# Turned pairs' first parts issued one tile later and behind the split, one block per turned copy, and the turned copy read ahead of the MLP's weights

## The chip, the cores and the metric

One NeuronCore of one Trainium2 chip runs the whole program. The metric is the device time of one execution in microseconds (us). Engines as the profile names them: PE is TensorE (matmuls and transposes by matmul), PEld its weight loads, DVE is VectorE, ACT is ScalarE, POOL is GpSimd, SP is SyncE, whose queue starts nearly all of this kernel's DMAs.

## The reference, cut to what matters

Two layers; in each, an FNet Fourier sublayer and an MLP, both with a LayerNorm ahead of them (the MLP with two, one inside the other).

```python
S, D, F = 2048, 576, 4608
def _A_ref(x, dft_seq_re, dft_seq_im, dft_hid_re, dft_hid_im):
    a = jnp.einsum("bsd,ed->bse", x, dft_hid_re)
    b = jnp.einsum("bsd,ed->bse", x, dft_hid_im)
    return jnp.einsum("ts,bse->bte", dft_seq_re, a) - jnp.einsum("ts,bse->bte", dft_seq_im, b)
def _B_ref(x, w1, b1, w2, b2):
    y = _layernorm(x)
    h = _gelu(jnp.einsum("bsd,df->bsf", y, w1) + b1)
    return jnp.einsum("bsf,fd->bsd", h, w2) + b2
x = A_x
for layer in range(2):
    x = x + _A_ref(_layernorm(x), ...)
    x = x + _B_ref(_layernorm(x), ...)
```

## The kernel before, in words

Every float32 product is made of three passes over a high and a low part of each operand (`PASSES`); "splitting" a tile is a copy to the high part on ACT and a subtraction for the low part on DVE (`split`). The large products use a seven-product block scheme (Strassen and Winograd's), so that sums of blocks are made ahead of the multiplication.

The order of all work is the order in which the program's lines run: there is no scheduler. Each engine has one queue and takes its instructions in that order; an instruction whose operand is not ready holds up all that stands behind it on its engine. SP's queue holds the DMA starts in the same way.

A layer has four parts one after the other: the sequence DFT, then for each half of the 2048 rows a **hidden stage** (function `hidden`: the hidden DFT, the residual sum, the norms and the turning of the result) and the MLP of that half (`mlp`). The hidden stage so occurs four times in the program. All that is changed is in it.

A hidden stage has eight tiles n = 0 to 7 of 128 rows. For a tile it

- loads the sequence DFT's result of tile n+2 (`h.load`, DMA `uv_mid`) and x;
- splits tile n+1 (`turn`, line 202 on ACT, 1152 columns, and line 199 on DVE): PE needs the high part for a tile's first four matmuls and the low part from the fifth on;
- lets PE run 54 matmuls (9 blocks k, 3 passes, 2 halves; line 209);
- adds the sum to x (line 196 on DVE), and makes the norm: `norms(n)` is a generator of three steps, the statistics (DVE, then POOL's lines 230 to 234), the normalising (line 253 on ACT), and adding b2 to x (line 196 on POOL). The caller places its steps with `next(ln)`: the second and the third stand in the next tile's iteration.

The MLP needs the normalised tiles turned (columns in partitions) and in seven block combinations, split again, in the array `y`. Tiles go in pairs j: tiles 0 and 1 (j = 0), 2 and 3 (j = 1), 4 and 5 (j = 2), and 6 and 7 by themselves. The ways of turning differ:

- Pairs 0 and 1 go **through DRAM**. `write_turned(j)` at the start of tile 2 or 4 transposes 32 by 32 blocks on DVE (line 206) and writes the block `raw` to DRAM (`y_mid`, two DMAs); `read_turned(j)` in tile 3 or 5 at k = 1 reads it back with four DMAs in another order. Then `first_parts(j)` makes the three combinations that are plain blocks (line 985: three copies on ACT, and five subtractions of line 199 on DVE), `turn_sums(j)` makes the block sums (four subtractions on POOL, in place), and `turn_parts(j)` the four combinations that are sums (three copies on ACT, three subtractions on DVE).
- Pair 2 is turned **by PE**: `turn_blocks`, called after tile 6, makes 8 transposes (line 959) and 4 more (line 962); then `first_parts(2)` and `turn_sums(2)`, the latter on DVE. PE's transposes of tile 5's blocks need tile 5's normalising.
- Tiles 6 and 7 are turned by PE in `turn_y` (line 1020) after tile 7, with the first part of the MLP's product (35 matmuls of 128x256) ahead of them on PE.

Where things stand in the iterations of the hidden stage before:

```python
                if n in (3, 5):
                    if k == 1:
                        read_turned(n // 2 - 1)
                    if k == 8:
                        first_parts(n // 2 - 1)
                if n in (4, 6):
                    if k == 1:
                        turn_sums(n // 2 - 2)
                    if k == 8:
                        turn_parts(n // 2 - 2)
```

So `first_parts(0)` is issued at the end of tile 3, ahead of tile 3's sum and of the split of tile 5 (start of tile 4), and `first_parts(1)` at the end of tile 5, ahead of the split of tile 7. The MLP's generator is started at the start of tile 5 (`next(mlp)` at n == NP - 3), which starts the reads of its first weights (`w_parts`): two in the first half of a layer, seven in the second.

The blocks: `t8` and `t9` of 8 x 288 columns each. `raw` is the front of `t8`. Both turned copies are read into `turned_x`, the front of `t9`; pair 2's turned copy lies in `t8` behind column 768. Tiles 4 and 5 are normalised into `t8`, tiles 6 and 7 into `t9`.

Of the kernel before, what the change touches and what calls it, by code (L numbers as in the profile page):

```python
# [15 lines left out]
P = 128  # L16
NT = S // P
DH = D // 2
NP = NT // 2
# [138 lines left out]
def spectral_mixer(ctx: ExitStack, tc: tile.TileContext, x, dh, c0, cs, w1, b1, w2, b2, out):  # L158
# [33 lines left out]
    def dma(dst, src):  # L192
        nc.sync.dma_start(dst, src)  # L193
# [682 lines left out]
    def hidden(h, mlp):  # L876
# [12 lines left out]
        y = Y(7, 5, TC)  # L889
        t8 = A.alloc(8 * DH, low=True)  # L890
        t9 = A.alloc(8 * DH, low=True)
        es, b2t = A.alloc(7 * 3 * 32, low=True), A.alloc(D, low=True)
        raw, turned_x = Block(A, t8.at, 4 * DH), Block(A, t9.at, 12 * P)
        dma(b2t(D), b2.to_broadcast([P, D]))

        def norms(n):

            tile_x = xv[:, :, order[n]]
            if n < 4:
                g = raw(9, 4, 32).rearrange("p g e i -> p e g i")  # L900
# [24 lines left out]
            if n < NP - 1:  # L925
                add(nc.gpsimd, tile_x, tile_x, b2t(2, DH))
            yield
# [8 lines left out]
        def read_turned(j):  # L936
            src = yd[j].rearrange("(q d) c f -> c d q f", q=4)
            for c in range(4):
                dma(turned_x(4, 3 * P)[32 * c:32 * c + 32], src[c])

        def rests(j):
            e = es(7, 3, 32)
            if j == 2:
                v = t8(8, DH)
                nc.scalar.activation(e[:, :4], v[:, 0:4, None, 2 * P:].to_broadcast([P, 4, 3, 32]), AF.Copy)
                return
            v = t9(8, DH)
            nc.scalar.activation(e[:, :, 1].bitcast(F32R), v[:, 1:8, 2 * P:], AF.Copy)
# [3 lines left out]
        def turn_blocks():  # L952


            v, x = t8(8, DH), t8(8 * DH)[:, 6 * P:].rearrange("p (b k t) -> p b k t", b=4, k=3)
            a, b = space(), space()
# [9 lines left out]
        def parts(j, e, i, high=True, low=True, engine=nc.vector):  # L966


            if j < 2:
                x = turned_x(4, 3, 4, 32).rearrange("p q f e t -> p f e q t")[:, :, e]  # L970
                yv = y[:, :, :, j * P:(j + 1) * P].rearrange("p i f (q t) -> p f i q t", q=4)[:, :, i]
# [6 lines left out]
            else:  # L978
                x = t8(8 * DH)[:, 6 * P:].rearrange("p (b k t) -> p b k t", b=4, k=3)[:, e]
                yv = y[:, i, :, j * P:(j + 1) * P]  # L980
# [13 lines left out]
        def turn_sums(j):  # L994
            if j < 2:
                x = turned_x(12, 4, 32).rearrange("p g e t -> p e g t")
            else:
                x = t8(8 * DH)[:, 6 * P:].rearrange("p (b k) -> p b k", b=4)
            b11, b12, b22, b21 = (x[:, k] for k in range(4))
# [9 lines left out]
        def turn_y():  # L1009
            v = t9(8, DH)  # L1010
            at = slice(3 * P, 4 * P)
            blocks = (1, 7, 6, 2, 3, 4, 5)
            for m, i0 in enumerate((2, 4, 0, 6)):
# [21 lines left out]
        for n in range(NP):  # L1035
# [19 lines left out]
            for k in range(KH):  # L1055
                if n == 0 and k == KH // 2:
                    drain(turn(1))
                if n in (3, 5):
                    if k == 1:
                        read_turned(n // 2 - 1)  # L1060
                    if k == 8:
                        first_parts(n // 2 - 1)
                if n in (4, 6):
                    if k == 1:
                        turn_sums(n // 2 - 2)
                    if k == 8:
                        turn_parts(n // 2 - 2)
                if k == 4:
# [33 lines left out]
        add(nc.gpsimd, tile_x, tile_x, b2t(2, DH))  # L1102
        for b in (*h.places, t8, t9, es, b2t):
            b.free()
# [369 lines left out]
```

## Time and profile before

| | |
|---|---|
| median of 3 runs | 2758.68 us (2756.53 to 2760.1) |
| profiled execution | 2756.53 us, the fastest of the three |
| its span, first to last instruction | 2754.7 us (1.8 us lie outside) |
| granted TensorE clock, mean | 0.983 |
| PE busy / DVE / ACT / POOL | 96% / 66% / 40% / 31% |
| idle time of PE ahead of line 959 / line 1020, four stages | 37.2 us / 12.9 us |
| idle time of PE for a low part (DVE line 199), whole program | 27.8 us |

How to read it: a PE at 96% leaves about 4% of gaps, and the program can gain no more from filling them than the gaps and what the lower clock costs behind them. The rows of a timeline are merged runs of equal instructions of one engine: start, duration of the run, engine and line, what is written from what, count, and in brackets the idle time of the engine just before and what ended it. Rows of SPq are DMA starts.

### The profile page before, as it was taken

What the parts mean: (1) busy time and instruction counts of PE and PEld (TensorE: products, weight loads), DVE (VectorE), ACT (ScalarE), POOL (GpSimd) and SP (SyncE); (2) the same over time, 40 slices, a digit from 0 to 9 for tenths busy, and PEclk for the clock granted to TensorE, in tenths of its full rate; (3) what the DMA queues carried; (4) which work ended last, traced back from release to release, by engine and by line L of the source; (5) the groups of instructions that cost most, each with busy time, mean ns of one, the idle gap of its engine ahead of it and who ended that gap; (6) DMA issues with size and microseconds to landing.
All of it is one profiled execution on the core that took longest, in us unless ns stands there. A gap on an engine that the chain in (4) does not pass through costs nothing.

```text
span 2754.7 us, 44664 instructions
## 1 busy us (share of the span) xinstructions
PE 2656.1 (96%) x17156; PEld 2486.7 (90%) x17156; DVE 1820.7 (66%) x2539; ACT 1103.8 (40%) x1817; POOL 845.1 (31%) x730
## 2 busy tenths in 40 slices
PE   9999997999999799999999999979999996999999
PEld 9999997888888788988899999978999996998988
DVE  8999975877776465556677777456555554655555
ACT  6555553544443243333354333334333322433331
POOL 6334334434442332222250000232222233321222
PEclk9999998999999899999999999989999998999999
DMA  5777785777778656666553333746666685666664
GB/s 176 250 251 247 244 269 178 257 269 275 264 270 304 166 157 195 193 202 218 160 207 131 123 125 122 211 140 196 193 192 193 194 260 143 189 193 197 190 197 154
DMA packets 236164, 557.47 MB, mean 202 GB/s; under 512 B 24352, under 2 KB 87840, under 8 KB 235808
## 3 DMA queue, kind: packets, MB, share of 16 engines
q1 hardware_dynamic: 222624, 524.53, 60.9%
q10 hardware_dynamic: 13328, 30.09, 2.9%
q8 instruction: 136, 2.23, 0.3%
q14 instruction: 76, 0.62, 0.1%
HBM read 436.16 MB, written 121.01 MB: 202 GB/s over the span
## 4 chain that ended last, share of the span: by engine, by line
PE 59%; DVE 2%; DMA 1%; SPq 1%; issue 1%; ACT 0%; POOL 0%; DVEq 0%; POOLq 0%; ACTq 0%
PE bank L209 59%; DVE R L199 1%; SPq L193 1%; DMA R<-w_parts 0%; DVE A L196 0%; DMA R<-uv_mid 0%; DMA A<-y_mid 0%; PE bank L1020 0%; DVE A L199 0%; POOL moments L230 0%; DVE moments L224 0%; DMA A<-uv_mid 0%; ACT A L253 0%; ACT R L985 0%; PE bank L1030 0%
## 5 line engine op out<-in xcount | busy, mean ns | idle before, releaser
L209 PE MATMUL bank<-R 128*128 128x288 f32 (+2 forms) x16972 | 2625.7, 316 | 40.5 <-DVE R L199 27.8
L209 PEld LDWEIGHTS bank<-R 128*128 128x128 f32 x16972 | 2456.9, 190 | 206.9 <-DVE R L199 33.2
L196 DVE TENSOR_TENSOR A<-bank,A 128x576 f32<-128x576 f32 (+3 forms) x808 | 567.9, 709 | 532.9 <-PE bank L209 439.3
L199 POOL TENSOR_TENSOR R<-A,R 128x512 fp32r<-128x512 f32 (+1 forms) x286 | 373.6, 1317 | 905.1 <-ACT R L1283 866.0
L199 DVE TENSOR_TENSOR R<-A,R 128x1024 fp32r<-128x1024 f32 (+7 forms) x555 | 524.7, 971 | 168.5 <-ACT R L985 123.4
L196 POOL TENSOR_TENSOR A<-A 128x576 f32<-128x576 f32 (+2 forms) x102 | 144.0, 1416 | 526.5 <-ACT A L693 340.5
L199 POOL TENSOR_TENSOR A<-A 128x384 f32<-128x384 f32 (+3 forms) x184 | 226.4, 1234 | 223.1 <-DVE R L199 95.4
L1222 ACT ACTIVATE bank<-bank,b1t 128x512 f32<-128x512 f32 (+1 forms) x224 | 144.9, 647 | 369.4 <-DVE bank L196 242.5
L1283 ACT ACTIVATE R<-A 128x512 fp32r<-128x512 f32 x288 | 177.0, 629 | 271.8 <-DVE A L199 123.6
L652 ACT ACTIVATE R<-A 128x1024 fp32r<-128x1024 f32 x196 | 206.3, 1054 | 106.6 <-PE bank L209 63.7
L196 DVE TENSOR_TENSOR bank<-bank,A 128x512 f32<-128x512 f32 (+1 forms) x228 | 152.3, 669 | 144.2 <-PE bank L209 143.2
L199 DVE TENSOR_TENSOR R<-bank,R 128x512 fp32r<-128x512 f32 x232 | 156.0, 675 | 4.8 <-ACT R L1283 4.2
L199 DVE TENSOR_TENSOR A<-A 128x1024 f32<-128x1024 f32 (+3 forms) x134 | 147.1, 1104 | 4.4
L1283 ACT ACTIVATE R<-bank 128x512 fp32r<-128x512 f32 x216 | 121.3, 595 | 29.9 <-PE bank L209 29.8
L1249 ACT ACTIVATE A<-bank 128x512 f32<-128x512 f32 (+1 forms) x76 | 43.7, 575 | 208.8 <-PE bank L209 208.6
L253 ACT ACTIVATE A<-A,moments 128x576 f32<-128x576 f32 (+2 forms) x90 | 57.6, 689 | 131.0 <-POOL moments L234 93.5
L230 POOL TENSOR_TENSOR moments<-moments,power 128x1 f32<-128x1 f32 x32 | 43.1, 1346 | 191.1 <-DVE moments L227 191.1
L199 DVE TENSOR_TENSOR A<-bank,A 128x512 f32<-128x512 f32 x144 | 97.9, 680 | 0.0
L279 ACT ACTIVATE R<-A 128x256 fp32r<-128x256 f32 x126 | 51.9, 412 | 64.6 <-DMA A<-in_w 19.7
L1222 ACT ACTIVATE A<-bank,b1t 128x512 f32<-128x512 f32 (+1 forms) x76 | 50.6, 666 | 62.6 <-DVE bank L196 62.6
L985 ACT ACTIVATE R<-A 128x384 fp32r<-128x384 f32 (+3 forms) x60 | 35.2, 643 | 90.8 <-DMA A<-y_mid 57.8
L206 DVE STREAM_TRANSPOSE A<-A 128x1152 f32<-128x1152 f32 x40 | 55.1, 1378 | 15.4 <-ACT A L253 12.4
(64 smaller groups left out, 610.4 us busy)
## 6 DMA issues: line engine op xcount, KB each, us to landing
R<-w_parts SPq DMA_DIRECT2D x504, 320.0 KB, 3.4
R<-w_parts SPq DMA_DIRECT2D x189, 576.0 KB, 3.8
A<-in_cs SPq DMA_DIRECT2D x112, 512.0 KB, 4.0
w_parts<-R SPq DMA_DIRECT2D x63, 576.0 KB, 5.0
w_parts<-R ACTq DMA_DIRECT2D x81, 320.0 KB, 3.6
uv_mid<-A SPq DMA_DIRECT2D x28, 576.0 KB, 3.1
w_parts<-R SPq DMA_DIRECT2D x45, 320.0 KB, 4.3
A<-in_w SPq DMA_DIRECT2D x72, 192.0 KB, 4.7
```

The costliest lines, as they stand in the source:

```text
L196: engine.tensor_tensor(dst, a, b, op=op)
L199: engine.tensor_tensor(dst, a, b, op=OP.subtract)
L206: nc.vector.transpose(block(2 * D), block(2 * D))
L209: nc.tensor.matmul(o, a, b, start=start, stop=stop, skip_group_check=True)
L230: nc.gpsimd.tensor_tensor(mv[:, 3:4], mv[:, 2:3], power[:, 0:1], op=OP.pow)
L253: nc.scalar.activation(dst, src, AF.Identity, bias=mv[:, 4:5], scale=mv[:, 3:4])
L279: nc.scalar.activation(t[:, 1:4:2], src[:, 0:3:2], AF.Copy)
L652: nc.scalar.activation(self.cells[t, i](2, NP, P)[:, 0], self.source(t, i), AF.Copy)
L985: nc.scalar.activation(dst, src, AF.Copy)
L1222: nc.scalar.activation(dst, src, AF.Gelu_apprx_tanh, bias=bias(f))
L1249: nc.scalar.activation(up, o, AF.Copy)
L1283: nc.scalar.activation(H[q, k](2, TC)[:, 0], src, AF.Copy)
```

## The change

What it does, in four edits:

1. `first_parts(j)` moves from the end of tile 3 (5) to the start of tile 4 (6), behind the split of tile 5 (7) and ahead of the normalising of tile 3 (5). `turn_sums(j)` moves from k = 1 of tile 4 (6) to just ahead of k = 0, which is the same place on POOL. `turn_parts(j)` moves from the end of tile 4 (6) to the start of tile 5 (7), behind the split of tile 6; for pair 1 there is no split there.
2. The two turned copies that come from DRAM get a block each (`xs[0]`, `xs[1]`); pair 2's copy has the block of pair 0's.
3. Tiles 6 and 7 are normalised into the block in which tiles 4 and 5 lay (`v8`, the front of which is `raw`); the back half of `v8`, for tile 7's sums, lies over pair 1's copy. The room is 4224 columns in place of 4608, so `es` and `b2t`, which are taken next, lie lower.
4. `next(mlp)` moves from the start of tile 5 to its k = 3, behind the DMAs of `read_turned(1)`.

```diff
-        t8 = A.alloc(8 * DH, low=True)
-        t9 = A.alloc(8 * DH, low=True)
+        t8 = A.alloc(4 * DH + 24 * P, low=True)
...
-        raw, turned_x = Block(A, t8.at, 4 * DH), Block(A, t9.at, 12 * P)
+        raw, v8 = Block(A, t8.at, 4 * DH), Block(A, t8.at, 8 * DH)
+        xs = [Block(A, t8.at + 4 * DH + k * 12 * P, 12 * P) for k in (1, 0, 1)]
...
-            elif n < 6:
-                v = t8(8, DH)
+            else:
+                v = v8(8, DH)
                 z = v[:, 0:2] if n % 2 else v[:, 2:4]
-            else:
-                v = t9(8, DH)
-                z = v[:, 0:2] if n % 2 else v[:, 6:8]
...
-                b12, b22, t1, t3, t2, t4, b11, b21 = (v[:, k] for k in range(8))
+                b12, b22, b11, b21, t1, t3, t2, t4 = (v[:, k] for k in range(8))
...
             if n:
                 drain(turn(n + 1))
+                if n in (4, 6):
+                    first_parts(n // 2 - 2)
+                if n in (5, 7):
+                    turn_parts(n // 2 - 2)
                 next(ln)
+                if n in (4, 6):
+                    turn_sums(n // 2 - 2)
             if n in (2, 4):
                 write_turned(n // 2 - 1)
             if n == 6:
                 rests(2)
-            if n == NP - 3:
-                next(mlp)
             o = space()
...
-                if n in (3, 5):
-                    if k == 1:
-                        read_turned(n // 2 - 1)
-                    if k == 8:
-                        first_parts(n // 2 - 1)
-                if n in (4, 6):
-                    if k == 1:
-                        turn_sums(n // 2 - 2)
-                    if k == 8:
-                        turn_parts(n // 2 - 2)
+                if n in (3, 5) and k == 1:
+                    read_turned(n // 2 - 1)
+                if n == NP - 3 and k == 3:
+                    next(mlp)
```

No instruction is added or taken away. What moves in the queues, in the first of the four hidden stages (the others have the same order but for the loads). First ACT, from the normalising of tile 2 to that of tile 5; L253 is normalising, L202 the split's copy (1152 columns), L985 the copies of first parts (3x128) and of turned sums (4x128). Before:

```order
L253 ACTIVATE A<-A,moments 128x2x4x32 x2
L253 ACTIVATE A<-A,moments 128x2x32
L985 ACTIVATE R<-A 128x3x128 x3
L202 ACTIVATE R<-A 128x1152
L253 ACTIVATE A<-A,moments 128x2x4x32 x2
L253 ACTIVATE A<-A,moments 128x64
L985 ACTIVATE R<-A 128x4x128 x3
L202 ACTIVATE R<-A 128x1152
L253 ACTIVATE A<-A,moments 128x576
L985 ACTIVATE R<-A 128x3x128 x3
L202 ACTIVATE R<-A 128x1152
L253 ACTIVATE A<-A,moments 128x576
```

With the change, at the same place on ACT (its line 980 is line 985 of before):

```order
L253 ACTIVATE A<-A,moments 128x2x4x32 x2
L253 ACTIVATE A<-A,moments 128x2x32
L202 ACTIVATE R<-A 128x1152
L980 ACTIVATE R<-A 128x3x128 x3
L253 ACTIVATE A<-A,moments 128x2x4x32 x2
L253 ACTIVATE A<-A,moments 128x64
L202 ACTIVATE R<-A 128x1152
L980 ACTIVATE R<-A 128x4x128 x3
L253 ACTIVATE A<-A,moments 128x576
L202 ACTIVATE R<-A 128x1152
L980 ACTIVATE R<-A 128x3x128 x3
L253 ACTIVATE A<-A,moments 128x576
```

Each group of part copies has changed places with the split that stood behind it. On DVE the subtractions move further, past the residual sum and the statistics too. At DVE's end of the stage, up to tile 7's sum (the last row); L224 to L227 are tile 6's statistics, `A<-A 128x384 x4` is `turn_sums(2)`. Before:

```order
L199 TENSOR_TENSOR R<-A,R 32x4x128
L199 TENSOR_TENSOR R<-A,R 128x4x128 x2
L196 TENSOR_TENSOR A<-bank,A 128x2x288
L224 BN_STATS moments<-A 128x6 x2
L225 BN_AGGR moments<-moments 128x2
L227 TENSOR_SCALAR moments<-moments 128x1
L199 TENSOR_TENSOR R<-A,R 32x2x128
L199 TENSOR_TENSOR R<-A,R 128x2x2x128
L199 TENSOR_TENSOR R<-A,R 32x128
L199 TENSOR_TENSOR R<-A,R 128x2x128
L199 TENSOR_TENSOR A<-A 128x384 x4
L196 TENSOR_TENSOR A<-bank,A 128x2x288
```

With the change, from tile 6's sum to tile 7's:

```order
L196 TENSOR_TENSOR A<-bank,A 128x2x288
L224 BN_STATS moments<-A 128x6 x2
L225 BN_AGGR moments<-moments 128x2
L227 TENSOR_SCALAR moments<-moments 128x1
L199 TENSOR_TENSOR R<-A,R 32x2x128
L199 TENSOR_TENSOR R<-A,R 128x2x2x128
L199 TENSOR_TENSOR R<-A,R 32x128
L199 TENSOR_TENSOR R<-A,R 128x2x128
L199 TENSOR_TENSOR A<-A 128x384 x4
L199 TENSOR_TENSOR R<-A,R 32x4x128
L199 TENSOR_TENSOR R<-A,R 128x4x128 x2
L196 TENSOR_TENSOR A<-bank,A 128x2x288
```

The subtractions of pair 1's turned sums (`32x4x128` and `128x4x128 x2`) have moved from ahead of tile 6's sum to between `turn_sums(2)` and tile 7's sum. Last SP, in tile 5's iteration, behind the write of pair 1's copy and tile 7's loads (`A<-y_mid` is the read of pair 1's copy, `R<-w_parts` the MLP's weights, `dh_parts` the hidden DFT's parts that are kept in DRAM, in the first stage alone):

```order
 L193 DMA A<-in_x 128x2x288
 L193 DMA dh_parts<-R 128x576 x2
-L193 DMA R<-w_parts 128x640 x2
-L193 DMA A<-y_mid 32x4x384 x4
+L193 DMA A<-y_mid 32x4x384 x4
+L193 DMA R<-w_parts 128x640 x2
 L193 DMA dh_parts<-R 128x576 x6
```

The read of the copy and the weights have changed places; in the second half of a layer seven weight reads stand there in place of two.

More of the change, by code (lines that the diff above doesn't have):

```diff
@@ L938, in read_turned @@
             for c in range(4):
-                dma(turned_x(4, 3 * P)[32 * c:32 * c + 32], src[c])
+                dma(xs[j](4, 3 * P)[32 * c:32 * c + 32], src[c])
         def rests(j):
-            e = es(7, 3, 32)
+            e, v = es(7, 3, 32), v8(8, DH)
             if j == 2:
-                v = t8(8, DH)
                 nc.scalar.activation(e[:, :4], v[:, 0:4, None, 2 * P:].to_broadcast([P, 4, 3, 32]), AF.Copy)
                 return
-            v = t9(8, DH)
             nc.scalar.activation(e[:, :, 1].bitcast(F32R), v[:, 1:8, 2 * P:], AF.Copy)
@@ L952, in turn_blocks @@
         def turn_blocks():
-            v, x = t8(8, DH), t8(8 * DH)[:, 6 * P:].rearrange("p (b k t) -> p b k t", b=4, k=3)
+            v, x = raw(4, DH), xs[2](4, 3, P)
             a, b = space(), space()
@@ L978, in parts @@
             else:
-                x = t8(8 * DH)[:, 6 * P:].rearrange("p (b k t) -> p b k t", b=4, k=3)[:, e]
+                x = xs[j](4, 3, P)[:, e]
                 yv = y[:, i, :, j * P:(j + 1) * P]
@@ L995, in turn_sums @@
             if j < 2:
-                x = turned_x(12, 4, 32).rearrange("p g e t -> p e g t")
+                x = xs[j](12, 4, 32).rearrange("p g e t -> p e g t")
             else:
-                x = t8(8 * DH)[:, 6 * P:].rearrange("p (b k) -> p b k", b=4)
+                x = xs[j](4, 3 * P)
             b11, b12, b22, b21 = (x[:, k] for k in range(4))
@@ L1009, in turn_y @@
         def turn_y():
-            v = t9(8, DH)
+            v = v8(8, DH)
             at = slice(3 * P, 4 * P)
-            blocks = (1, 7, 6, 2, 3, 4, 5)
+            blocks = (1, 3, 2, 4, 5, 6, 7)
             for m, i0 in enumerate((2, 4, 0, 6)):
@@ L1102, in hidden @@
         add(nc.gpsimd, tile_x, tile_x, b2t(2, DH))
-        for b in (*h.places, t8, t9, es, b2t):
+        for b in (*h.places, t8, es, b2t):
             b.free()
```

2 lines of the change are left out of this document (1 added, 1 removed).

## The prediction

> **What bounds the kernel now.** The page has PE at 96% of the span, so I read first what PE waits for. In the waits of PE (engine, line, releaser: us in total, times, longest) three rows hold most of what is left:
>
> ```profile
> PE bank L959 <- ACT A L253: 37.2, 4, 13.0
> PE bank L209 <- DVE R L199: 27.8, 16, 3.4
> PE bank L1020 <- issue: 12.9, 4, 3.6
> ```
>
> The first and the third come four times each, once in each hidden stage; the longest of the second lie there too. The timeline of PE in the first stage shows where, and the last row, from the second stage, what an unhindered stretch behind a short gap looks like:
>
> ```profile
> 389.24 28.52 PE L209 MATMUL bank<-R 128*128 128x288 f32 x212 [0.16 <-DVE R L199]
> 418.51 0.80 PE L209 MATMUL bank<-R 128*128 128x288 f32 x4 [0.76 <-ACT R L202]
> 422.24 8.97 PE L209 MATMUL bank<-R 128*128 128x288 f32 x54 [2.93 <-DVE R L199]
> 434.62 9.39 PE L209 MATMUL bank<-R 128*128 128x288 f32 x50 [3.41 <-DVE R L199]
> 449.80 1.54 PE L959 MATMUL bank<-ident,A 128*128 128x128 f32 x6 [5.57 <-ACT A L253]
> 451.85 12.51 PE L209 MATMUL bank<-R 128*128 128x288 f32 x89
> 468.13 2.79 PE L1020 MATMUL bank<-ident,A 128*128 128x128 f32 x12 [3.54 <-issue]
> ...
> 882.74 42.61 PE L209 MATMUL bank<-R 128*128 128x288 f32 x318 [1.52 <-DVE A L196]
> ```
>
> A matmul takes 28.52 / 212 = 0.1345 us, a tile of 54 so 7.26 us. Tile 4 ends at 417.76. Tile 5 runs its first four matmuls late and then waits 2.93 us for its low part, tile 6 waits 3.41 us for its own, the six transposes behind tile 5's blocks wait 5.57, and tile 7's transposes 3.54. Next I ask each releaser what it waited for: ACT, DVE and SP in the same stretch.
>
> ```profile
> 416.06 1.35 ACT L985 ACTIVATE R<-A 128x384 fp32r<-128x384 f32 x3 [6.78 <-DMA A<-y_mid]
> 417.31 1.15 ACT L202 ACTIVATE R<-A 128x1152 fp32r<-128x1152 f32 x1
> 441.76 1.35 ACT L985 ACTIVATE R<-A 128x384 fp32r<-128x384 f32 x3 [5.35 <-DMA A<-y_mid]
> 448.88 0.87 ACT L253 ACTIVATE A<-A,moments 128x576 f32<-128x576 f32 x1 [4.71 <-POOL moments L234]
> 454.68 1.01 ACT L963 ACTIVATE A<-bank 128x1024 f32<-128x1024 f32 x1
> 456.20 1.26 ACT L985 ACTIVATE R<-A 128x768 fp32r<-128x768 f32 x2
> ...
> 417.02 1.93 DVE L199 TENSOR_TENSOR R<-A,R 32x256 fp32r<-32x256 f32 x5 [10.17 <-ACT R L985]
> 420.83 1.36 DVE L199 TENSOR_TENSOR R<-A,R 128x1152 fp32r<-128x1152 f32 x1
> 424.63 1.38 DVE L206 STREAM_TRANSPOSE A<-A 128x1152 f32<-128x1152 f32 x1 [2.45 <-ACT A L253]
> 458.85 1.86 DVE L199 TENSOR_TENSOR R<-A,R 32x256 fp32r<-32x256 f32 x4
> 460.80 3.54 DVE L199 TENSOR_TENSOR A<-A 128x384 f32<-128x384 f32 x4
> 464.26 0.75 DVE L196 TENSOR_TENSOR A<-bank,A 128x576 f32<-128x576 f32 x1
> ...
> 402.32 1.26 SPq L193 DMA_DIRECT2D y_mid<-A  x2
> ```
>
> It is one cause. At 416.06 pair 0's turned copy lands; ACT had stood 6.78 us for it and DVE 10.17, because `first_parts(0)` is at the head of both queues. Only behind it come tile 5's split (ACT 417.31, DVE 420.83, a tile late), tile 3's sum and norm, and with that norm the transposing of pair 1 (424.63). So pair 1's copy lands late too (441.76), and again ACT and DVE stand before it; tile 5's sum, statistics and normalising (448.88) come behind it, and PE's transposes wait for these. Each wait feeds the next.
>
> **The change, step by step.** I call R1 the landing of pair 0's copy, T4 PE's end of tile 4. Both stay where they are, since nothing ahead of them moves. The rows for the other stages (T4 is the start of the PE row less its wait: 925.35, 1791.95, 2285.68):
>
> ```profile
> 926.17 0.79 PE L209 MATMUL bank<-R 128*128 128x288 f32 x4 [0.82 <-ACT R L202]
> 1792.39 0.79 PE L209 MATMUL bank<-R 128*128 128x288 f32 x4 [0.44 <-ACT R L202]
> 2285.85 0.80 PE L209 MATMUL bank<-R 128*128 128x288 f32 x4 [0.17 <-ACT R L202]
> ...
> 910.32 1.25 SPq L193 DMA_DIRECT2D y_mid<-A  x2
> 1777.71 1.24 SPq L193 DMA_DIRECT2D y_mid<-A  x2
> 2271.27 1.24 SPq L193 DMA_DIRECT2D y_mid<-A  x2
> ...
> 923.71 1.35 ACT L985 ACTIVATE R<-A 128x384 fp32r<-128x384 f32 x3 [6.86 <-DMA A<-y_mid]
> 1789.93 1.35 ACT L985 ACTIVATE R<-A 128x384 fp32r<-128x384 f32 x3 [6.47 <-DMA A<-y_mid]
> 2283.39 1.35 ACT L985 ACTIVATE R<-A 128x384 fp32r<-128x384 f32 x3 [6.20 <-DMA A<-y_mid]
> ```
>
> First, tile 5's split no longer stands behind R1. Its load is ahead of the copy's read in SP's queue and so lands before it; at the latest the split then starts at R1 less nothing, 416.06, its copy is done at 417.2 and PE wants it at 417.76. Tile 5's wait goes.
>
> Second, tile 6's split. On DVE stand ahead of it now the first parts' subtractions (they end 0.96 + 1.93 = 2.89 after R1), the transposing of pair 1 (1.38), then tile 4's sum and statistics (before, 418.95 to 420.83: 1.88). Its low part ends at R1 + 2.89 + 1.38 + 1.88 + 1.36 = R1 + 7.51. PE needs it at T4 + 7.26 + 0.54 (four matmuls). The slack is 2.0, 1.9, 2.3 and 2.6 us in the four stages. Tile 6's wait goes, but this is the thinnest cover: a copy that lands 2 us later brings it back. Tile 3's normalising, on ACT behind the first parts, is hidden by the 2.89 (its nearest row is the 0.87 of a whole tile; in three pieces it takes somewhat more).
>
> Third, R2, the landing of pair 1's copy. Its write starts at R1 + 4.27 (2.89 + 1.38), against 426.01 before, 9.95 after R1. From the write's start to the landing SP now issues just what it issues for pair 0: write, the next tile's load, x, the kept parts, read. So I take pair 0's own row in each stage, write to landing: 13.74, 13.39, 12.22, 12.12 us. R2 is 434.1, 941.4, 1806.4, 2299.8. Separate blocks make this possible (the read need not wait until pair 0's copy has been used up), and the weight reads, now behind, come later by the read's issue only; the MLP wants them a tile later, so I cost that at nothing.
>
> Fourth, tile 5's normalising. Its sum no longer waits for R2: PE ends tile 5 at about R1 + 9, and sum, statistics (1.88) and POOL's steps (before, from 446.53 to 448.88: 2.35) leave it ready by R1 + 13 to 16 even behind the turned sums; R2 is R1 + 16 to 18. So it follows the first parts' copies on ACT and ends at R2 + 1.35 + 0.87: 436.3, 943.6, 1808.6, 2302.0. PE is through tile 6 and two transposes (0.38) at T4 + 14.9: 432.7, 940.3, 1806.9, 2300.6. It still waits, 3.6, 3.3, 1.8 and 1.4 us, for what is late next, R2.
>
> Fifth, the end of the stage. From the normalising PE needs 2.05 (449.80 to 451.85) for the rest of the transposes, 89 matmuls x 0.1345 = 11.97 and 0.38: 14.4 us. DVE needs 1.54 (transposes), 1.52 (454.68 to 456.20), 0.63, 1.86, 3.54, then pair 1's turned sums, which now stand here (1.93, as the five subtractions), and 3.87 from tile 7's sum to PE's going on (464.26 to 468.13): 14.9 us. So DVE ends last by 0.5; moving the turned sums behind `turn_sums(2)` costs what it is given there, but they had been ahead of tile 6's sum on the same queue, so nothing is added.
>
> Sixth, the clock. Behind the waits before line 1020 the granted clock is down for a while; four windows of 8 us from that point (us, PE busy, PEclk):
>
> ```profile
> 468.13:476.13 8.00, 8.00 (x56) 0.83 0.55 155
> 980.96:988.96 8.00, 8.00 (x48) 0.67 0.01 2
> 1842.47:1850.47 8.00, 8.00 (x54) 0.79 0.07 9
> 2340.49:2348.49 8.00, 8.00 (x53) 0.79 0.05 8
> ```
>
> That costs 8 x (0.17 + 0.33 + 0.21 + 0.21) = 7.4 us in all, 1.84 for a wait of about 3 us. A wait of 1.52 was followed by 318 matmuls at full speed (42.61 us). So I charge 1.84 for the new waits of 3.6 and 3.3 us, nothing for 1.8 and 1.4, and give back the 7.4, since the waits at line 1020 shrink to about half a us. The Trainium skill, TensorE: Matmul & The Clock Gate, Part 1, says that the clock halves only after at least one whole idle window of about 3.4 us. The trace disagrees: in each of these four windows the clock is below 1, with waits of 3.2 us on average in front (12.9 / 4). By the page's rule the 3.3 would cost nothing, and the second stage would go on at DVE's 958.5, 1.3 us sooner.
>
> Line 1020 so goes on at 452.5 (PE's 436.3 + 14.4 + 1.84), 959.8, 1823.5 (DVE's 1808.6 + 14.9) and 2316.9. Against 468.13, 980.96, 1842.47 and 2340.49 this saves 15.6, 21.2, 19.0 and 23.6: 79.4 us, with the clock 86.8. Against it stands one cost that the trace doesn't show: the blocks lie lower, and in the first stage the MLP's raw weights are loaded over some of them, so these loads may wait for a later last reader. Bounds: 0, and the 3.87 from tile 7's sum to line 1020; since ACT has other work there I take 1. The sum is 85.8: 2756.53 becomes 2670.7 for an execution like the profiled one, which was the fastest of three; the median was 2.15 higher, so I predict 2673.
>
> **Rivals.** *The copy lands as late as pair 1's did.* Pair 1's rows before, in the first and the second stage, with two and seven weight reads ahead of the copy:
>
> ```profile
> 933.79 1.24 SPq L193 DMA_DIRECT2D y_mid<-A  x2
> 954.47 1.35 ACT L985 ACTIVATE R<-A 128x384 fp32r<-128x384 f32 x3 [10.30 <-DMA A<-y_mid]
> ```
>
> Write to landing is 20.7 us here and 15.75 in the first stage (426.01 to 441.76): 7.3 and 2.0 more than pair 0's. If the weights, though behind, still share the engines with the copy, all four landings are 2 us later at least (8 us), and the waits of 1.8 and 1.4 grow past 3 and cost clock (3.7): 2685; at 7.3 in the two stages with seven reads, 2695. For it: the reads start right behind the copy. Against it: pair 0's copy also has a tile's load right behind it. The Trainium skill, DMA: Bandwidth & Descriptors, Queues, rings and completion order, says that an engine takes descriptors in ring order, but completion is not first in, first out per issuing engine; the rows of pair 0 can't tell how much of that there is.
>
> *Quicker.* If R2 comes 2 us sooner (the earlier write meets less traffic), the waits of 3.6 and 3.3 fall under the clock's mark and all four shrink: 8 + 3.7 us, but DVE and PE are then close: 2661.
>
> *No earlier copy.* If R2 stays at its old time, the waits before line 959 end only as much sooner as sum, statistics and POOL fall away behind it, 448.88 + 0.87 - (441.76 + 2.22) = 5.8 us a stage; four stages and the 7.4 make 30.6: 2728. Nothing but an unseen wait of the write speaks for it.
>
> *Slower.* The weight reads now wait on SP behind a read that waits for DRAM. PE wants the first weights at R2 + 2.2 + 2.05 + 7.26, 11.5 us after R2, and they are started right behind the read that lands at R2, so each us that they land later than R2 + 11.5 costs up to 4 us in the program. It decides at 11.5 + 86 / 4 = 33 us after R2, where the longest landing above is 20.7 from a write's start on; at 35 us the time would be 2673 + 4 x 23.5 = 2767.
>
> **How the numbers follow.** Forecast 0.70, late copy 0.14, quicker 0.10, no earlier copy 0.03, slower 0.03. The range 2658 to 2696 holds the first three with their bounds (about 2 us either way for the forecast's landing in each stage). The cases of the other sign hold 0.03. A measurement of this kernel tells about 0.2% (5 us) from no change: faster 0.96, same 0.01, slower 0.03.
>
> **What the profile of the changed kernel would show.** most of PE's 27.8 us of waits for DVE L199 gone, with no wait longer than 1 us at tiles 5 and 6; the first parts' ACT rows twice in each stage behind a split, the second about 16 to 18 us after the first (25.7 now in the first stage); the wait before the transposes 1 to 4 us in place of 5.6 to 13; tile 7's transposes behind a wait under 1 us; and a mean clock near 0.995. Wrong it is if a wait comes back at tile 6 (the slack of 2 us was too thin), if the second copy lands more than 18 us after the first, or if PE stands at the MLP's first weights.

## The result, and the profile after

| | before | changed |
|---|---|---|
| median | 2757.61 us (2755.09 to 2760.1, 4 runs) | 2684.32 us (2681.87 to 2685.48, 4 runs) |
| ratio | | 0.9733, 95% interval 0.9716 to 0.975 |
| span of the profiled execution | 2754.7 us | 2682.8 us |
| granted clock, mean | 0.983 | 0.994 |

The change saves 73.3 us by the medians; the forecast was 85.8, and the time lies 11.3 us above the 2673 forecast. From the waits of PE in the changed kernel (us in total, times, longest; lines 954 and 1015 are 959 and 1020 of before; ... stands for rows left out):

```profile
PE bank L954 <- ACT A L253: 16.7, 4, 6.5
PE bank L209 <- DVE R L199: 8.6, 11, 1.6
...
PE bank L209 <- DMA R<-w_parts: 2.4, 4, 1.3
...
PE bank L1015 <- issue: 0.4, 1, 0.4
```

The three waits that the forecast spoke of fell from 77.9 us to 25.7. PE's timeline in the first hidden stage shows what is left:

```profile
387.71 41.63 PE L209 MATMUL bank<-R 128*128 128x288 f32 x311
429.18 0.38 PE L954 MATMUL bank<-ident,A 128*128 128x128 f32 x2
436.05 1.54 PE L954 MATMUL bank<-ident,A 128*128 128x128 f32 x6 [6.48 <-ACT A L253]
...
438.09 9.12 PE L209 MATMUL bank<-R 128*128 128x288 f32 x62
448.72 5.24 PE L209 MATMUL bank<-R 128*128 128x256 f32 x27 [1.51 <-DVE R L199]
453.80 1.69 PE L1015 MATMUL bank<-ident,A 128*128 128x128 f32 x14
```

One row now runs through tiles 3 to 6: the waits of tiles 5 and 6 are gone. The wait before the block transposes is there, 6.48 us. Tile 7's transposes no longer wait; instead there is a wait that the kernel before did not have, 1.51 us ahead of 128x256 matmuls. These are the MLP's second product step, which reads pair 1's turned sums, and DVE makes these last. The landings of the two copies, on ACT:

```profile
414.38 1.35 ACT L980 ACTIVATE R<-A 128x384 fp32r<-128x384 f32 x3 [5.17 <-DMA A<-y_mid]
433.89 1.35 ACT L980 ACTIVATE R<-A 128x384 fp32r<-128x384 f32 x3 [5.83 <-DMA A<-y_mid]
```

They are 19.5 us apart (25.7 before). To size the steps I cut each stage in three pieces by the starts of matmuls in the trace: A, from tile 3's start to the third block transpose (line 954), behind its wait; B, from there to the third transpose of line 1015; C, from there to 200 matmuls behind the first transpose of line 1015. Sums over the four stages, in us (the last three columns are experiments below):

| piece | before | forecast | changed | changed again (e10) | b2 later (e6) | b2 later (e11) |
|---|---|---|---|---|---|---|
| A | 196.2 | 128.0 | 133.4 | 127.4 | 128.4 | 128.9 |
| B | 73.3 | 62.2 | 70.8 | 69.6 | 58.7 | 59.5 |
| C | 148.2 | 140.8 | 144.5 | 145.1 | 147.2 | 147.6 |
| sum | 417.8 | 331.0 | 348.7 | 342.1 | 334.3 | 336.0 |

Of the 71.9 us between the spans 69.1 lie in these pieces; 2.8 lie in the first 400 us, which the change doesn't touch, and which took 400.05 to 405.8 us from one profiled execution to another, so these 2.8 are luck. B and C are best read together, for where PE is through B sooner it waits the longer in C: 221.5 us before, 203.0 forecast, 215.3 and 214.7 (e10) measured, 206.0 (e6) and 207.1 (e11) with b2 later.

### The profile page after: what moved, and what is told of

Read it like the earlier page. It is cut to its first block, busy times and chain, and to the rows that moved or that the text cites. A ratio compares the mean times of both kernels' runs of the same rounds, so it can differ in the third digit from the quotient of the medians.

```text
span 2682.8 us, 44678 instructions
## 1 busy us (share of the span) xinstructions
PE 2636.6 (98%) x17156; PEld 2470.3 (92%) x17156; DVE 1829.7 (68%) x2539; ACT 1103.5 (41%) x1817; POOL 853.2 (32%) x730
## 3 DMA queue, kind: packets, MB, share of 16 engines
q8 instruction: 136, 2.23, 0.3%
## 4 chain that ended last, share of the span: by engine, by line
PE 82%; DVE 6%; DMA 5%; ACT 2%; SPq 2%; issue 2%; POOL 1%; ACTq 0%; DVEq 0%; POOLq 0%
PE bank L209 82%; DVE R L199 3%; DMA A<-y_mid 2%; SPq L193 2%; DVE A L199 1%; DMA w_parts<-R 1%; DMA R<-w_parts 1%; DMA A<-in_x 1%; DVE A L196 1%; DMA R<-uv_mid 0%; POOL A L199 0%; DMA A<-uv_mid 0%; DMA A<-in_w 0%; DVE A L206 0%; ACT R L980 0%
## 5 line engine op out<-in xcount | busy, mean ns | idle before, releaser
L199 DVE TENSOR_TENSOR R<-A,R 128x1024 fp32r<-128x1024 f32 (+7 forms) x555 | 536.0, 992 | 85.2 <-ACT R L980 40.6
L253 ACT ACTIVATE A<-A,moments 128x576 f32<-128x576 f32 (+2 forms) x90 | 57.6, 689 | 80.0 <-POOL moments L234 53.4
L280 ACT ACTIVATE R<-A,power,middle 128x128 fp32r<-128x128 f32 x126 | 60.7, 482 | 0.0
```

Of the source, the lines that this page charges most:

```text
L199: engine.tensor_tensor(dst, a, b, op=OP.subtract)
L253: nc.scalar.activation(dst, src, AF.Identity, bias=mv[:, 4:5], scale=mv[:, 3:4])
L280: nc.scalar.activation(t[:, 2], src[:, 1], AF.Identity, bias=power[:, 2:3], scale=middle)
```

## The experiments

The first four ran together, and the kernel before took 2753.34 us (2750.5 to 2755.45, 7 runs) beside them; by the ratio 0.9733 the changed kernel takes 2680 there. Each is the changed kernel with the edit shown.

**e1, the weights ahead of the read again (edit 4 undone).**

```diff
+            if n == NP - 3:
+                next(mlp)
...
-                if n == NP - 3 and k == 3:
-                    next(mlp)
```

> The changed kernel with its fourth edit undone: the MLP's first weight reads stand ahead of the second turned copy's read in SP's queue again, all else as changed. Theory (the second copy's landing, R2, sets the rest of the stage, and what is queued ahead of it on SP and the DMA engines moves R2): R2 later by 1.5 to 2 us in stages 1 and 3 (two reads) and by 4 to 7 in stages 2 and 4 (seven reads), the wait before the block transposes longer by as much, time 2684 + 11 to 18 = 2695 to 2702 us. Rival (the gain is the order on ACT and DVE alone, the reads are hidden anyway): same R2, 2684 within 5 us.

2702.97 us (2701.18 to 2705.93), ratio 0.982 (0.9805 to 0.9835): 23 us of the gain are gone, more than the 11 to 18 expected. The wait before the transposes is 30.4 us in all. The copies' landings in its fourth stage, with seven weight reads:

```profile
2241.35 1.35 ACT L980 ACTIVATE R<-A 128x384 fp32r<-128x384 f32 x3 [3.20 <-DMA A<-y_mid]
2266.56 1.35 ACT L980 ACTIVATE R<-A 128x384 fp32r<-128x384 f32 x3 [11.50 <-DMA A<-y_mid]
```

25.2 us apart here (17.8 with the reads behind), 18.4 in the third stage with two (16.4). Edit 4 makes the copy land sooner, most of all where there are seven reads.

**e2, the parts at their old places (edit 1 undone).**

```diff
-                if n in (4, 6):
-                    first_parts(n // 2 - 2)
-                if n in (5, 7):
-                    turn_parts(n // 2 - 2)
...
+                    if k == 8:
+                        first_parts(n // 2 - 1)
```

> The changed kernel with its first edit undone: first parts, turned sums and turned parts at the places of before, with the new blocks and the weight reads behind the copy. Theory: the waits of tiles 5 and 6 for their low parts come back whole (2.4 to 3.4 us each), since ACT and DVE stand before the first copy again; the second copy lands 2 us (stages 1, 3) to 7 us (stages 2, 4) sooner than before, which the wait before the block transposes gives back: 2758 - 18 = 2740 us, between 2735 and 2745. Rival (blocks and read order make the larger part of the gain): under 2715 us.

2734.17 us (2732.32 to 2736.34), ratio 0.9933 (0.9918 to 0.9947): 54 us of the gain are gone, and 19 are left for edits 2 to 4. PE's timeline in the first stage has the old waits at tiles 5 and 6 and before the transposes of line 1015:

```profile
419.24 8.97 PE L209 MATMUL bank<-R 128*128 128x288 f32 x54 [2.93 <-DVE R L199]
431.63 8.43 PE L209 MATMUL bank<-R 128*128 128x288 f32 x50 [3.41 <-DVE R L199]
...
463.36 2.72 PE L1015 MATMUL bank<-ident,A 128*128 128x128 f32 x12 [3.14 <-issue]
```

2.93 and 3.41 are to the hundredth what stood there before. The order on ACT's and DVE's queues is the larger part of the change.

**e3, one block for both copies (edit 2 undone).**

```diff
-        xs = [Block(A, ...) for k in (1, 0, 1)]
+        xs = [Block(A, ...) for k in (0, 0, 1)]
```

> The changed kernel with one block for both turned copies from DRAM (pair 2's copy in the other). Theory: the second read must wait until pair 0's turned sums are cut on DVE, which in the changed kernel end 2.1, 3.2, 3.3 and 2.6 us after the read's start in the four stages; R2 and all behind it later by that, sum 11 us, time 2695 us (2690 to 2699). Rival (a block of its own costs and brings nothing, because the write to DRAM must land first anyway): 2684 within 4 us.

2685.73 us (2683.14 to 2688.21), ratio 0.9759 (0.9743 to 0.9776). Its interval overlaps that of the changed kernel: the own block is worth between nothing and about 7 us, less than I expected. The wait that I expected is there: SP starts the second read 8.2, 8.2, 8.2 and 7.6 us after the copy's write, and 5.9, 4.9, 4.8 and 4.8 in the changed kernel (e10). But the copy landed only 1.5, 0.7, 1.9 and 1.7 us later than in e10, counted from the first copy. Piece A, 132.7 us, is 5.3 more than in e10, and as long as in the first profile of the changed kernel, whose copies landed late too; one execution's spread is as large as this edit.

**e4, tile 5's normalising ahead of pair 1's first parts (and tile 3's ahead of pair 0's).** Only after seeing the result did I ask what bounds the first wait: ACT normalises tile 5 behind the copy's three parts, though the moments can be ready sooner. In tile 4 the edit also puts the transposing and writing of pair 1 ahead of pair 0's first parts.

```diff
-                if n in (4, 6):
-                    first_parts(n // 2 - 2)
...
                 next(ln)
-                if n in (4, 6):
-                    turn_sums(n // 2 - 2)
...
+            if n in (4, 6):
+                first_parts(n // 2 - 2)
+                turn_sums(n // 2 - 2)
```

> The changed kernel with the normalising (and, in tile 4, the transposing and writing of pair 1) ahead of the first parts on ACT and DVE, so that neither tile 3's nor tile 5's normalising stands behind a copy that has yet to land. Theory (PE's wait before the block transposes is nothing but tile 5's normalising queued behind R2 on ACT): the wait, 16.7 us in all, falls under 4 us; the second copy is written about 3 us sooner and R2 comes about 3 us sooner; DVE's chain to tile 7's transposes then starts at R2 + 1.35 in place of R2 + 3.7, some 5.7 us sooner a stage: 2684 - 23 = 2661 us (2655 to 2668). Rival (the statistics or POOL are as late as R2): the wait stays above 10 us and the time within 8 us of 2684.

2686.64 us (2685.59 to 2686.85), ratio 0.9759 (0.9744 to 0.9773): no gain. In PE's waits the one before the transposes halved to 8.1 us (neither the 4 of the theory nor the 10 of its rival), and the second product step's (in the first of these rows) took it back:

```profile
PE bank L209 <- DVE R L199: 20.3, 12, 5.3
PE bank L954 <- ACT A L253: 8.1, 4, 2.3
```

So the stage's end hangs on the chain to pair 1's turned sums, and PE, sooner through the transposes, waits there. Nor did this chain start sooner, though the copy's write started 2.2 to 3.5 us sooner after tile 3's start than in the first profile of the changed kernel: pair 1's first parts now stand on ACT behind tile 5's normalising, which waits for POOL's moments, and began 31.5 to 31.9 us after tile 3's start in all four stages (29.2 to 33.5 and, in e10, 28.6 to 30.9 in the changed kernel). The next four take that chain apart, beside a kernel before of 2751.86 us (2750.68 to 2757.27, 9 runs); by the ratio the changed kernel takes 2678 there.

**e5, pair 1's sums cut ahead of `turn_sums(2)`**, between it and `first_parts(2)`.

```diff
-                if n in (5, 7):
-                    turn_parts(n // 2 - 2)
+                if n == 5:
+                    turn_parts(0)
...
+                turn_parts(1)
```

> All numbers are for a session in which the kernel before takes 2753.3 us, so that the changed one (ratio 0.9733) takes 2680. Edit: the parts of pair 1's turned sums stand ahead of turn_sums(2) on DVE, not between turn_sums(2) and tile 7's sum. Theory: DVE's chain from the copy to tile 7's sum is what ends the stage; this edit only changes its order. PE's wait at the MLP's second product step (5.9 us in the four stages) goes, but a wait of 0.5 to 1 us a stage comes back ahead of line 1015, and the time moves by no more than 4 us: 2676 to 2684. Rival: the wait at the second product step is a loss of its own, the order of the parts is the fault, and the wait goes with the clock that it costs: 2670 to 2674.

2681.39 us (2680.11 to 2686.23), ratio 0.9743 (0.9729 to 0.9756): the same as the changed kernel. In PE's waits the one at the second step gave way to one at line 1015:

```profile
PE bank L954 <- ACT A L253: 12.3, 4, 3.9
PE bank L1015 <- issue: 8.8, 4, 2.5
PE bank L209 <- DVE R L199: 6.8, 10, 2.5
```

The order within DVE's chain is worth nothing; its length is what counts. The rival, that the dependence itself is the loss, falls.

**e6, POOL's additions of b2 for tiles 5 and 6 behind the product.**

```diff
-            if n < NP - 1:
+            if n < 5:
...
-        tile_x = xv[:, :, order[NP - 1]]
-        add(nc.gpsimd, tile_x, tile_x, b2t(2, DH))
+        for n in (5, 6, 7):
+            tile_x = xv[:, :, order[n]]
+            add(nc.gpsimd, tile_x, tile_x, b2t(2, DH))
```

> All numbers are for a session in which the kernel before takes 2753.3 us, so that the changed one takes 2680. Edit: POOL's additions of b2 to tiles 5 and 6 (line 196, 1.4 and 1.9 us at the stage's end) are made behind the MLP's product, as tile 7's already is. Theory: DVE and POOL hold each other up there (DVE's subtraction of 128x512 elements took 1.80 us beside POOL's addition, 0.56 to 0.68 alone), so DVE's chain to tile 7's sum ends 1.5 to 2.3 us sooner in each stage and the waits of PE behind it shrink: 2673 to 2677. Rival: DVE's long subtractions come from their operands or from ACT, not from POOL; the rows stay as long and the time is 2680 within 3.

2673.66 us (2669.5 to 2678.18), ratio 0.9712 (0.9697 to 0.9726). DVE's subtractions at the stage's end (line 199; the mean is in ns), first of the changed kernel, window 440 to 449.3 us, then of this one, 436.6 to 444.2:

```profile
L199 DVE TENSOR_TENSOR R<-A,R 128x512 fp32r<-128x512 f32 x3 | 2.7, 929 | 0.0
L199 DVE TENSOR_TENSOR R<-A,R 32x512 fp32r<-32x512 f32 x1 | 1.8, 1800 | 0.0
L199 DVE TENSOR_TENSOR R<-A,R 32x128 fp32r<-32x128 f32 x1 | 1.4, 1428 | 0.0
```

```profile
L199 DVE TENSOR_TENSOR R<-A,R 128x512 fp32r<-128x512 f32 x3 | 2.7, 930 | 0.0
L199 DVE TENSOR_TENSOR R<-A,R 32x512 fp32r<-32x512 f32 x1 | 0.7, 684 | 0.0
L199 DVE TENSOR_TENSOR R<-A,R 32x128 fp32r<-32x128 f32 x1 | 0.3, 283 | 0.0
```

The same two instructions took 1.80 and 1.43 us beside POOL's additions and 0.68 and 0.28 without them, 2.3 us less. DVE's chain is 1.8 us shorter (9.17 to 7.37; its rows stand in the next section), since a third subtraction (32x256), now beside POOL's sums, took 0.89 us in place of 0.42. Piece B fell from 70.8 to 58.7 us, below the forecast's 62.2. That DVE was held by POOL is shown.

**e7, pair 1's sums made on DVE in place of POOL.**

```diff
-            g = nc.gpsimd if j < 2 else nc.vector
+            g = nc.gpsimd if j < 1 else nc.vector
```

> All numbers are for a session in which the kernel before takes 2753.3 us, so that the changed one takes 2680. Edit: turn_sums(1) is made on DVE (four subtractions of 128x384, 0.56 us each when DVE is undisturbed, 2.2 in all), not on POOL (4.4 us). Theory: POOL's four hold up DVE's subtractions of the first parts and tile 5's and 6's steps behind them; with them gone DVE's own rows there (3.72 us for four of 32x256) shrink to 1.9 or less, tile 5's moments come 4.4 us sooner on POOL so that the wait before the block transposes shrinks to what the second copy's landing leaves (about 2 us a stage in place of 4.2), and DVE's chain ends 1 to 2 us sooner a stage: 2672 to 2678. Rival: DVE is the busier of the two there, so 2.2 us more on it end the stage 2 us later: 2684 to 2690.

2686.54 us (2684.09 to 2688.42), ratio 0.9756 (0.9742 to 0.9769): the rival's number. The wait before the transposes, expected at about 8 us in all, is 13.3. DVE's four subtractions are 2.34 us in place of POOL's 4.4, but they stand ahead of tile 6's sum on DVE, whose b2 addition then falls on `turn_sums(2)`; PE's waits for line 199 are 16.1 us (8.6 and, in e10, 10.7 in the changed kernel). I had counted POOL's time as gained and not asked what the 2.34 push back.

**e8, e4 to e7 together.**

> All numbers are for a session in which the kernel before takes 2753.3 us, so that the changed one takes 2680. Edit: the three edits of this call together (parts of pair 1's turned sums ahead of turn_sums(2), b2 for tiles 5 and 6 behind the product, turn_sums(1) on DVE), and tile 5's normalising ahead of pair 1's first parts, which had cut the wait before the block transposes from 16.7 to 8.1 us and given it back at the second product step. Theory: with POOL out of DVE's way both ends of the stage come sooner, and what the normalising gains is no longer given back: PE's waits in the four stages fall from 26 us to under 12, the clock's losses behind them too, 2660 to 2670. Rival: the chain from the second copy's landing to tile 7's sum stays the bound whatever stands on POOL: 2676 to 2684.

2678.79 us (2678.54 to 2680.66), ratio 0.9731 (0.9718 to 0.9745): the rival's. DVE's chain, longer by the sums, ends behind PE again, as PE's waits show:

```profile
PE bank L1015 <- DVE A L199: 10.3, 4, 2.6
PE bank L954 <- ACT A L253: 7.8, 4, 1.9
```

The last three ran beside a kernel before of 2753.86 us (2750.84 to 2757.27, 9 runs).

**e10, the changed kernel once more.** No edit.

> The changed kernel itself, once more beside the next two, so that the three are compared on one chip. Its ratio to the kernel before was 0.9733; the same is expected, 0.972 to 0.975. Open is how much of the 5.3 us by which the waits before the block transposes were longer than forecast is a property of the order, and how much the landing of pair 1's copy in one execution: in five profiles with the copy's write at the same place PE's going on came 31.2 to 35.7 us after tile 3's start. If it is the execution, the four stages differ here by 1 us or more from those of the first profile; if it is the order, they repeat within 0.5 us.

2680.9 us (2678.29 to 2684.58, 5 runs), ratio 0.9743 (0.973 to 0.9756). Piece A is 127.4 us in this profile, 6.0 less than in the first; of the single stages 2.6, 1.5, 0.6 and 1.2 less. The program is the same, so this is the execution: in the first stage the second copy landed 18.2 us after the first, not 19.5, and the first copy itself 1.4 us sooner. On ACT:

```profile
412.99 1.36 ACT L980 ACTIVATE R<-A 128x384 fp32r<-128x384 f32 x3 [4.38 <-DMA A<-y_mid]
431.17 1.35 ACT L980 ACTIVATE R<-A 128x384 fp32r<-128x384 f32 x3 [4.51 <-DMA A<-y_mid]
```

**e11, b2 later once more.** The edit of e6.

> The kernel with b2 for tiles 5 and 6 behind the product, once more beside the changed one. Theory (POOL holds up DVE at the stage's end): from the block transposes' going on to the third transpose of line 1015 it took 14.7 us in all four stages against 17.0 to 18.0 with the change alone, and again should; the 12 us so saved in the stages, with the clock that the shorter waits keep, make it 8 to 15 us faster than the changed kernel beside it. Rival: the first profile was the fastest of its runs and its copies landed early; the difference of the medians is then 5 us or less.

2678.65 us (2672.74 to 2683.6, 4 runs), ratio 0.9728 (0.9714 to 0.9742). Its piece B repeats (59.5), but beside the changed kernel it is 2.2 us faster by the medians, with overlapping intervals, as the rival had it. The profiled execution was the fastest of its four, as in e6, e9 and e10, so the pieces show their kernels at their best, and piece C took 3 us more than in the changed kernel, whose cause I did not follow. At the stage's end the gain is clear: B and C took 206.0 and 207.1 us in e6 and e11, and 214.5 to 215.3 in the five profiles with POOL's additions at their place and the same order of first parts (the changed kernel, e1, e3, e5 and e10). That e6's edit makes the whole kernel faster is not shown; the two ratios beside the two of the changed kernel speak for about 5 us.

**e9, e4 and e6 together.**

> Edit: b2 for tiles 5 and 6 behind the product, and tiles 3's and 5's normalising ahead of the first parts. Ahead of the product's second step the normalising first had given its gain back because DVE, slowed by POOL, was the later one. Theory: with POOL's additions gone DVE's chain is 3 us shorter, so that of the 1 to 2 us a stage that the wait before the block transposes loses a part stays: 0 to 6 us faster than the kernel with b2 later alone. Rival: DVE's chain from the copy to tile 7's sum already ends with PE there (its waits at line 1015 and the second step are under 1 us), so that a sooner PE only waits longer at line 1015: the same within 3 us.

2678.66 us (2677.91 to 2681.58), ratio 0.9731 (0.9718 to 0.9745): the rival's number, at another place than it said. What stands last is the chain through POOL: ACT copies pair 1's sums behind POOL's four subtractions, and PE waits for them at the second product step:

```profile
440.34 1.67 ACT L980 ACTIVATE R<-A 128x512 fp32r<-128x512 f32 x3 [3.71 <-POOL A L199]
```

```profile
444.74 5.09 PE L209 MATMUL bank<-R 128*128 128x256 f32 x27 [3.09 <-DVE R L199]
```

From pair 1's first parts POOL's sums (4.7 us) and their cutting lead to the second product step. As in e4 these first parts stand behind tile 5's normalising (they began at 432.61, 31.5 us after tile 3's start), so normalising first speeds the transposes and not this chain. No version beats the changed kernel by more than the measurement can tell.

## Why the prediction was right, and where it was short

The forecast case came true in kind, but the saving fell short of it; the time is 11.3 us above 2673. Two of the three signs that were to show it wrong appeared, both in the first stage and both small: the second copy came over 18 us after the first (19.5, and 18.2 in e10), and PE stood at the MLP's first weights (1.26 us). The wait before the transposes, expected at 1 to 4 us, was 6.48 and 4.51 in two stages of the first profile.

**First and second (the splits of tiles 5 and 6): right.** Both waits are gone, and e2 brings them back.

**Third (R2): right in kind, and in size within what executions differ by.** Forecast between the landings were 18.0, 17.7, 16.5 and 16.4 us; the first profile has 19.5, 18.0, 16.4 and 17.8, the second (e10) 18.2, 17.7, 16.2 and 17.3; the fourth stage alone is later by about 1 us in both. The measured 2684 is also the number of the late-copy rival (2685), but by chance: it wants all four landings 2 us later. The late copy is e1, and there the two stages with seven reads pay the more, as that rival had it. That the weights' later start costs nothing was wrong by a little: in the first stage PE now waits 1.26 us for them, 0.79 with the reads ahead again (e1).

**Fourth (the wait before the transposes): right, but for the late landings of the first profile.** Forecast 3.6, 3.3, 1.8 and 1.4 us; measured 6.48, 4.51, 2.21 and 3.45, and 3.90, 2.97, 1.60 and 2.23 in e10. R1 was to stay where it was; in the first profile it came 1.1, 0.6, 0.3 and 0.4 us later after tile 3's start than before, and R2 with it. Piece A was to save 68.2 us and saved 62.8 and 68.8.

**Fifth (the end of the stage): the step that failed.** Piece B was to save 11.1 us and saved 2.5 and 3.7; B and C together are 12 us longer than forecast. I added DVE's rows of before to 14.9 us as if their durations belonged to them; what they stand beside changed. DVE now makes pair 1's first parts, `turn_sums(2)` and the turned sums while POOL makes its own sums and adds b2. The rows of the changed kernel, DVE and then POOL:

```profile
440.04 3.72 DVE L199 TENSOR_TENSOR R<-A,R 32x256 fp32r<-32x256 f32 x4 [1.30 <-ACT R L980]
443.79 2.34 DVE L199 TENSOR_TENSOR A<-A 128x384 f32<-128x384 f32 x4
446.16 3.11 DVE L199 TENSOR_TENSOR R<-A,R 32x512 fp32r<-32x512 f32 x3
```

```profile
441.29 1.88 POOL L196 TENSOR_TENSOR A<-A 128x576 f32<-128x576 f32 x1
...
445.97 1.44 POOL L196 TENSOR_TENSOR A<-A 128x576 f32<-128x576 f32 x1 [0.98 <-ACT A L253]
```

3.72 + 2.34 + 3.11 = 9.17 us, where I had 1.86 + 3.54 + 1.93 = 7.33. Without POOL's two additions (e6) the same rows take 3.05 + 2.33 + 1.99 = 7.37:

```profile
436.68 3.05 DVE L199 TENSOR_TENSOR R<-A,R 32x256 fp32r<-32x256 f32 x4 [0.73 <-ACT R L980]
439.77 2.33 DVE L199 TENSOR_TENSOR A<-A 128x384 f32<-128x384 f32 x4
442.14 1.99 DVE L199 TENSOR_TENSOR R<-A,R 32x512 fp32r<-32x512 f32 x3
```

The 3.54 of before already held one such stretch, which I took for the operation's own time. Nor had I seen that the MLP's second product step reads the turned sums, so that 27 matmuls (3.74 us at full clock in e10) follow on the chain's end in place of tile 7's sum; e5 shows that this by itself is worth nothing. With POOL's two additions gone (e6, e11) piece B takes 14.6 to 15.5 us a stage, near the 14.4 and 14.9 forecast, and 8 to 9 of the 12 us are back; the other 3 to 4 stay open.

The Trainium skill, SBUF — State Buffer, Who interferes with whom, says that a VectorE instruction with two operands in SBUF contends with a GpSimd instruction that reads SBUF, and that the one that comes second stands still until the first has ended. The trace agrees: the 32x512 subtraction began at 446.16, POOL's addition ended at 445.97 + 1.44 = 447.41, and the subtraction ended at 446.16 + 1.80 = 447.96, 0.55 us later, where the whole instruction takes 0.68 alone. Tile 6's residual sum, which has one operand in PSUM (`A<-bank,A`), ran beside POOL's subtractions in its usual 0.75 us:

```profile
436.70 0.75 DVE L196 TENSOR_TENSOR A<-bank,A 128x576 f32<-128x576 f32 x1
```

```profile
436.92 4.41 POOL L199 TENSOR_TENSOR A<-A 128x384 f32<-128x384 f32 x4 [5.96 <-DMA dh_parts<-R]
```

**Sixth (the clock): half right, and it did not decide the stage's end.** Piece C was to save 7.4 us and saved 3.7 and 3.1. That a wait of 1.5 us costs no clock was taken from one row; windows of 8 us in the changed kernel, behind the two waits of the first stage, the two of the second and the first of the third (us; PE, PEld, DVE, ACT and POOL busy with counts; PEclk; DMA share; GB/s):

```profile
436.05:444.05 8.00, 8.00 (x49) 7.96 (x50) 6.50 (x12) 4.93 (x8) 6.82 (x7) 0.77 0.78 306
448.72:456.72 8.00, 8.00 (x54) 7.78 (x55) 7.27 (x17) 4.33 (x9) 2.80 (x4) 0.79 0.00 1
930.29:938.29 8.00, 8.00 (x47) 7.96 (x48) 6.50 (x13) 4.94 (x8) 6.82 (x7) 0.73 0.34 132
942.97:950.97 8.00, 7.27 (x54) 6.24 (x55) 7.28 (x17) 3.35 (x9) 2.81 (x4) 1.00 0.09 35
1774.18:1782.18 8.00, 8.00 (x50) 7.96 (x51) 6.59 (x12) 4.94 (x8) 6.82 (x7) 0.79 0.34 128
```

Waits of 1.51 and 2.21 us were followed by 0.79, one of 1.21 by 1.00. (The prediction's average of 3.2 us hides that two of its four waits were 3.54 and 3.58; these shorter ones show better that less than 3 us can cost clock.) But neither wait's clock sets the stage's end. Behind the first wait PE stands at the second step anyway. Behind the second, e10 has a stage at the lower clock (27 matmuls in 5.21 us) and one at full clock (3.74 us):

```profile
937.91 5.21 PE L209 MATMUL bank<-R 128*128 128x256 f32 x27 [1.57 <-DVE R L199]
...
949.15 6.08 PE L209 MATMUL bank<-R 128*128 128x256 f32 x42 [0.36 <-ACT A L1242]
...
2258.15 3.74 PE L209 MATMUL bank<-R 128*128 128x256 f32 x27 [1.62 <-DVE R L199]
...
2262.49 1.78 PE L1015 MATMUL bank<-ident,A 128*128 128x128 f32 x12 [0.38 <-issue]
...
2265.45 1.04 PE L1025 MATMUL bank<-ident,A 128*96 128x128 f32 x7 [0.35 <-DVE R L199]
...
2269.38 5.85 PE L209 MATMUL bank<-R 128*128 128x256 f32 x41 [0.38 <-ACT A L1242]
```

From the first of these rows to the last it is 11.24 us in the one stage and 11.23 in the other: the quicker PE waits at the transposes instead. B and C together took 53.1 us in both, and 53.1 to 53.3 in the last three stages of all five profiles named under e11, at either clock. So I could not add the clock's 7.4 us to the end of DVE's chain: where DVE ends last, the slower PE cost nothing here.

The 1 us for loads over the lower blocks has no row of its own in the changed kernel and stays open. The other sign never came near.

## What to carry to other kernels

A duration from a trace belongs to an instruction and to what runs beside it: when work on VectorE with both operands in SBUF is moved, look at what GpSimd does at the new place, and at what it did at the old one. Where an in-order queue waits for a DMA, first leave behind the instruction that waits only what nobody else waits for, and start other large reads behind the one that is waited for; here that was worth 54 and 23 us. When a wait is halved and the time stands still, ask which chain ends last at the same place before shortening the wait further.

## What the runs showed of the hardware that I had not expected

- A subtraction on VectorE with both operands in SBUF took 0.28 or 0.68 us alone and 1.43 or 1.80 us where GpSimd was adding in SBUF at the same time.
- The same program landed a copy through DRAM 18.2 us after the one ahead of it in one execution and 19.5 in another, and single executions of one kernel spread by up to 11 us (e11: 2672.74 to 2683.6).
- How long a wait must be for the clock to drop is no fixed number here: behind 1.60 us (e10), 1.94 us (e4, first stage), 2.84 us (e6, second stage) and 3.17 us (e2, second stage) the 8 us window had 1.00, behind 1.51 us and 1.94 us (e4, third and fourth stage) 0.79.
